# Causal mask of the last twelve head pairs through masked copies of the gate sums, and a new planned order

## The chip, the cores and the metric

The kernel runs on one core of one Trainium2 chip. The metric is the device time of one execution in microseconds (us); the time before is the median of three runs.

## The reference

Two parts follow one another. The first is attention with a forget gate (batch 8, 8 heads, 576 positions, head size 64), the second a gated feed-forward block (4608 tokens, model width 512, inner width 1536):

```python
scores = scale * np.matmul(q, k.transpose(0, 1, 3, 2))
cum = np.cumsum(np.log(np.clip(f, 0.0001, 1.0)), axis=-1)
decay = cum[:, :, :, None] - cum[:, :, None, :]
scores = np.where(causal, -1000000000.0, scores + decay)
scores = scores - np.max(scores, axis=-1, keepdims=True)
attn = np.exp(scores)
attn = attn / (np.sum(attn, axis=-1, keepdims=True) + 1e-09)
attn_out = np.matmul(attn, v)
x = attn_out, heads joined, 4608 x 512
out = (silu(x @ w_gate) * (x @ w_val)) @ w_out
```

`causal` is true above the diagonal: a query sees no later key.

## The kernel before

**The tiles of the work.** Two heads of one batch form a pair; pairs 0 to 31 go through attention one after another, four pairs to a batch of 576 tokens. A pair's 576 queries are nine blocks of 64 rows; the two heads of a pair lie one above the other in the 128 partitions. Block i needs keys 0 to 64(i+1). The nine blocks form two groups: g=0 is blocks 0 to 3, g=1 is blocks 4 to 8.

**Attention of a pair, step by step.** K and Q are loaded (`kf`, `qf`, two buffers each), cast to bf16 with Q scaled by -1/8 (`kb`, `qb`, lines 451, 453; 530 to 534 for the first four pairs), transposed by TensorE (lines 467, 546) and copied out of PSUM to `kt` and `qz` (lines 479, 481; 559, 561). Then line 594 multiplies queries and keys into `sp` (PSUM, two banks), one matmul for each block, or two where a block needs more than 512 columns. **The causal mask** is a second matmul behind it, line 598: the identity as weights times a 128x64 `mask` that holds 1e9 above the diagonal, added to the last 64 columns of the block. VectorE then adds the gate sums `cb` to the scores and keeps the row minimum in one instruction (line 622, `tensor_tensor_reduce` with add and min, into `t` and `tm`; with the signs turned, the minimum stands for the maximum). A reading of its accumulator follows each. ScalarE takes the exponent and the row sum (line 642), VectorE the reciprocal of the sum (lines 656 to 660), GpSimd scales the rows to bf16 `pk` (line 678). `pk` is transposed by TensorE for pairs 0 to 7 (line 708, out of PSUM at 713) and by a DMA for the rest, and line 734 multiplies by V; line 758 writes the result into the ring `xT`.

**The feed-forward block.** Twelve tiles of 256, 256, seven times 512, 256, 128 and 128 tokens. For each tile line 816 makes 96 gate and value matmuls, lines 822 to 827 the activation (one ScalarE and two VectorE instructions of 512 columns per step), line 844 the output matmuls, 851 or 853 the copy to `ot` and 856 the store. A tile can start when all four pairs of its batch have written its tokens to `xT`. `xT` is a ring of `NRING` tokens, and a pair's result waits until the tile whose tokens it overwrites has been through line 816.

**What sets the order.** No engine's order is written out by hand. `Plan.order` takes every operation with its engines, costs, readers and writers, plays the kernel through on a model of engines, buffers and transfers, always starts next what can start first (ties by `prio`), and the instructions are issued on each engine in the order that comes out. Costs in the plan so change no instruction, only its place and sometimes its engine. Transfers are modelled on two wires, one for loads issued by SP and ACT, one for loads issued by GpSimd (POOL). `STARTUP` lists the first loads in order: `pN` the first 256 positions of K and Q (part A) for pairs N and N+1, or the whole K and Q of pair N from 4 on; `kN` and `qN` the other 320 positions (part B); `cN` gate sums; `vBC` chunk C of V of batch B; `wg`, `wv`, `wo` weights. `AHEAD` and `BEHIND` chain a load to one some places in front of it. `HEAD` gives the order of the first eight score groups (pair, group): 00 10 20 30 11 01 31 21. `NUDGE` shifts the priority of single units: aP.G attention of pair P group G, fT and oT the gate and output parts of tile T, qP the preparation of pair P, vB the V of a batch.

**What lies ready in the code.** From pair `MFROM` on, line 598 is left out; `copies` makes `cm`, the sum of `cb` and the mask for all nine diagonal blocks in one 128x576 add on GpSimd or VectorE, and `scores` adds `cb` to the columns left of the diagonal block and `cm` to the diagonal block, two instructions for a block where line 622 made one. `MFROM` is 32 here, so no pair does so. `TWO` sets how the two minima would join: apart with a small GpSimd instruction behind, or chained, the second addition starting from the first one's minimum. Block 8 is over 512 columns wide and so is cut in front of its diagonal block already: its second line-622 instruction is chained, for every pair.

Of the kernel before, what the change touches and what calls it, by code (L numbers as in the profile page):

```python
# [8 lines left out]
F32 = mybir.dt.float32  # L9
# [11 lines left out]
class Op:  # L21
    __slots__ = ("n", "engs", "fn", "reads", "writes", "prio", "lat", "dma", "deps", "start", "end", "eng", "after", "holds", "bias", "ring")

    def __init__(self, n, engs, fn, reads, writes, prio, lat, dma, after, holds):
        self.holds = list(holds)
# [7 lines left out]
class Plan:  # L33
# [24 lines left out]
    def op(self, engs, fn, reads=(), writes=(), prio=0.0, lat=80, dma=0, after=(), holds=()):  # L58
        o = Op(len(self.ops), engs, fn, list(reads), list(writes), prio, lat, dma, list(after), holds)
        self.ops.append(o)  # L60
        return o

    def order(self):
# [7 lines left out]
        for o in self.ops:  # L71
            deps = {d.n: d for k in o.reads for d in writers[k] if d is not o}
# [21 lines left out]
        wire = {True: 0, False: 0}  # L94
# [41 lines left out]
        while ready:  # L136
# [63 lines left out]
def kernel(  # L200
# [11 lines left out]
    nc = tc.nc  # L212
# [16 lines left out]
    NRING = 2560  # L229
# [10 lines left out]
    MFROM = 32  # L240
# [5 lines left out]
    TWO = True  # L246
# [9 lines left out]
    BEHIND = 6  # L256
# [4 lines left out]
    SLACK = 400  # L261
# [3 lines left out]
    STARTUP = "p0 f9 k0 p2 wv0 wg0 c0 v01 q1 q0 wv2 wg2 c1 v02 v00 k2 v04 c3 q2 wv4 v03 wg4 q3 c2 p4 v11 c4 wg8 wv8 c5 v14 p5 v13 v12 p6 c7 v10 c6 wo0 wo4 wo8 p7"  # L265
# [3 lines left out]
    NUDGE = "a5.0:-2 a8.0:1 a13.0:-1 a15.0:-2 a17.0:-2 a18.0:1.5 a22.0:2.5 a23.0:-1 a25.1:-1 a26.1:-1.5 f1:-2 f5:9 f7:0.5 o3:-4.5 o4:-0.5 o6:-8 o7:-3 q8:-2 q13:-3.5 q20:-2 q23:2 q25:4 q26:3.5 q30:-2"  # L269
# [33 lines left out]
    bufs("t", [P, S], F32, 4)  # L303
    for i in range(0, NB, 2):
        bufs(f"e{i}", [P, QB * (i + 2)], F32, 2)
# [59 lines left out]
    def gates(key, parts, np_, prio):  # L365
        x = lambda: pl.buf(key)[0:np_, :]
        for n, (a, z, src) in enumerate(parts):
            loads["f", key, n] = pl.op({"SP": 600}, lambda e, a=a, z=z, src=src: nc.sync.dma_start(out=pl.buf(key)[a:z, :], in_=src),
                                       (), [(key, 0)] + [key] * (n == 0), prio + n * .01, dma=570)
# [8 lines left out]
    for p in range(NDIRECT):  # L378
# [4 lines left out]
          [("fa", 3)], ["cum_dram"], -120, dma=570, lat=0, holds=["fa"])  # L383
# [31 lines left out]
    def load_pair(p):  # L415
# [5 lines left out]
        for name, src, pr in (("k", k, 0), ("q", q, .1)):  # L421
# [4 lines left out]
                (), [(name + "f", p)], (-99 + 3 * p if p < NPB else s - SOON) + pr, dma=1060, after=[sums[p - BACK, 0 if p - BACK >= NPB else 1]] if p >= NPB else [])  # L426
# [545 lines left out]
```

## Time and profile before

| | |
|---|---|
| median of three runs | 418.94 us |
| lowest and highest | 418.35 and 420.63 us |
| span of the profiled execution, first to last instruction | 417.2 us |
| TensorE matmul busy | 398.3 us, 95% of the span |
| VectorE, ScalarE, GpSimd busy | 79%, 74%, 60% |
| mean granted TensorE clock | 0.996 |

The profiled execution has no other time on its page than its span; the median of the runs is 1.7 us above it, and that is taken for what lies around the span. PE is TensorE's matmul row, PEld its weight loads, DVE VectorE, ACT ScalarE, POOL GpSimd, SP the engine that issues most transfers. A PE row's duration runs from issue to the end of the pipeline, so rows overlap; what a matmul takes of the stream is the distance from its start to the next start. The same holds of DVE rows, less strongly.

### The profile page before, as it was taken

Reading aid. Unit: us, or ns where it says so; the run is one execution under the profiler, and the core shown is the slowest. Engines: PE = TensorE matmul, PEld = TensorE weight load, DVE = VectorE, ACT = ScalarE, POOL = GpSimd, SP = SyncE. Lnnn points to the kernel's source line nnn. Section 1 sums busy time; section 2 is a strip of 40 time slices with the busy share of each in tenths; the row PEclk is TensorE's granted clock in tenths of the full one; section 3 lists DMA queues with packets and bytes.
Section 4 is the critical chain, followed back from the end, with each engine's and each line's share of the span. In section 5 each row is a group of like instructions: output and inputs, shape, how many; then the busy total and the mean of one; then the engine's idle time right before and its main releaser. Section 6 shows DMA issues by size and latency. Waiting matters only on the chain.

```text
span 417.2 us, 9955 instructions
## 1 busy us (share of the span) xinstructions
PE 398.3 (95%) x3250; PEld 232.3 (56%) x3296; DVE 328.9 (79%) x1065; ACT 310.3 (74%) x872; POOL 251.7 (60%) x459
## 2 busy tenths in 40 slices
PE   1979999999999999999999999999999999999996
PEld 0636878665555555555555554555555444457675
DVE  5688999999998899989897797798967764565232
ACT  4798999989995999899999984798996533232221
POOL 7589698987887897976968678267773400000000
PEclk9998999999999999999999999999999999999999
DMA  9999979695999999899999999848999211000211
GB/s 183 253 210 225 190 135 252 159 234 141 200 229 215 264 218 236 203 232 222 228 234 218 240 221 223 194 116 190 221 217 186 55 37 50 25 27 25 77 52 52
DMA packets 144004, 71.83 MB, mean 172 GB/s; under 512 B 117904, under 2 KB 131728, under 8 KB 143952
## 3 DMA queue, kind: packets, MB, share of 16 engines
q1 hardware_dynamic: 137568, 65.95, 71.1%
q0 software_dynamic: 5808, 4.72, 7.6%
q10 hardware_dynamic: 576, 0.52, 0.5%
q8 instruction: 26, 0.43, 0.4%
q14 instruction: 26, 0.21, 0.3%
HBM read 46.65 MB, written 9.58 MB: 135 GB/s over the span
## 4 chain that ended last, share of the span: by engine, by line
PE 86%; DVE 4%; issue 1%; ACT 0%
PE gv L816 43%; PE gv L844 22%; PE sp L594 9%; PE tx L734 6%; PE tx L467 3%; PE sp L598 2%; PE gv L708 2%; DVE t L622 1%; DVE pT L713 1%; DVE hh L827 1%; DVE th L824 1%; DVE qz L481 1%; DVE kt L481 0%; ACT ot L851 0%; DVE tm L622 0%
## 5 line engine op out<-in xcount | busy, mean ns | idle before, releaser
L622 DVE CUSTOM_DVE_ANT_0 t<-sp,cb 128x320 f32<-128x320 f32 (+7 forms) x288 | 130.4, 475 | 12.1 <-PE sp L598 8.6
L678 POOL TENSOR_SCALAR pk<-e,lr 128x128 bf16<-128x128 f32 (+3 forms) x190 | 100.5, 533 | 61.8 <-DVE lr L660 16.5
L816 PE MATMUL gv<-xT,wg 128*128 128x512 bf16 (+2 forms) x563 | 110.6, 327 | 0.8
L816 PE MATMUL gv<-xT,wv 128*128 128x512 bf16 (+2 forms) x562 | 109.3, 324 | 0.9
L844 PE MATMUL gv<-wo,hh 128*128 128x512 bf16 (+1 forms) x425 | 104.2, 373 | 0.8
L824 DVE SCALAR_TENSOR_TENSOR th<-th,gv 128x512 f32<-128x512 f32 x108 | 73.9, 684 | 39.3 <-ACT th L822 38.3
L822 ACT ACTIVATE th<-gv 128x512 f32<-128x512 f32 x108 | 64.1, 594 | 44.0 <-PE gv L816 43.1
L642 ACT ACTIVATE e<-t,tm 128x576 f32<-128x576 f32 (+4 forms) x160 | 88.7, 556 | 8.9 <-DVE tm L622 8.3
L827 DVE TENSOR_TENSOR hh<-th,gv 128x512 bf16<-128x512 f32 x108 | 73.7, 685 | 8.7 <-PE gv L816 4.9
L642 ACT ACTIVATE eo<-t,tm 128x128 f32<-128x128 f32 (+3 forms) x128 | 71.1, 556 | 4.7 <-DVE tm L622 2.9
L594 PE MATMUL sp<-kt,qz 128*128 128x448 bf16 (+6 forms) x320 | 71.9, 293 | 1.5 <-DVE tm L622 1.4
L678 POOL TENSOR_SCALAR pk<-eo,lr 128x128 bf16<-128x128 f32 (+3 forms) x127 | 67.6, 532 | 5.4 <-DVE lr L660 3.1
L816 PEld LDWEIGHTS <-wg 128*128 128x128 bf16 x576 | 49.8, 98 | 35.7
L816 PEld LDWEIGHTS <-wv 128*128 128x128 bf16 x576 | 48.9, 98 | 33.7 <-issue 0.3
L844 PEld LDWEIGHTS <-hh 128*128 128x128 bf16 x444 | 39.9, 98 | 39.0
L598 PE MATMUL sp<-mask,ident 128*128 128x64 bf16 x288 | 48.0, 197 | 0.0
L594 PEld LDWEIGHTS <-qz 128*128 128x128 bf16 x320 | 30.9, 100 | 20.9 <-DVE tm L622 0.9
L851 ACT ACTIVATE ot<-gv 128x512 f32<-128x512 f32 (+1 forms) x31 | 17.9, 580 | 27.1 <-PE gv L844 26.2
L598 PEld LDWEIGHTS <-ident 128*128 128x128 bf16 x288 | 27.2, 100 | 12.6 <-issue 1.9
L734 PE MATMUL tx<-pT,vt 128*64 128x320 bf16 (+4 forms) x448 | 29.6, 266 | 1.9 <-DVE pT L713 1.3
L451 POOL TENSOR_SCALAR qb<-qf 72x1024 bf16<-72x1024 f32 x28 | 29.1, 1041 | 3.1 <-DMA qf<-in_q_dram 2.0
L642 ACT ACTIVATION_READ_ACCUMULATOR e<-t,tm 128x1 f32 x160 | 30.6, 192 | 0.0
(69 smaller groups left out, 389.0 us busy)
## 6 DMA issues: line engine op xcount, KB each, us to landing
out_dram<-ot SPq DMA_DIRECT2D x35, 256.0 KB
vf<-in_v_dram SPq DMA_DIRECT2D x32, 256.0 KB
cb<-cum_f SPq DMA_DIRECT2D x56, 144.0 KB
kf<-in_k_dram SPq DMA_DIRECT2D x28, 288.0 KB
qf<-in_q_dram SPq DMA_DIRECT2D x28, 288.0 KB
wo<-in_moe_w_out_dram POOLq DMA_DIRECT2D x3, 512.0 KB, 10.8
vf<-in_v_dram SPq DMA_DIRECT2D x8, 128.0 KB
wv<-in_moe_w_val_dram POOLq DMA_DIRECT2D x2, 512.0 KB, 8.4
```

The lines of the kernel that those rows point to most:

```text
L451: eng[e].tensor_scalar(dst, src, -scale, 1.0, op0=ALU.mult, op1=ALU.mult)
L594: nc.tensor.matmul(sp[:, o:o + z - a], qz[:, i, :, :].rearrange("p h r -> p (h r)"), kt[:, a:z], start=True, stop=not last or p >= MFROM)
L598: nc.tensor.matmul(sp[:, o - QB:o], ident, mask, start=False, stop=True)
L622: nc.vector.tensor_tensor_reduce(out=pl.buf(tk)[:, a:z], in0=pl.buf(sk)[:, o:o + z - a], in1=pl.buf(("cm", p))[:, i, :] if own else pl.buf ...
L642: nc.scalar.activation(pl.buf(ek)[:, :L], pl.buf(tk)[:, :L], AF.Exp, bias=pl.buf(("tm", p, g))[:, 0, i:i + 1], scale=-1.0, accum_out=pl.bu ...
L678: eng[e].tensor_scalar(dst, src, r, 1.0, op0=ALU.mult, op1=ALU.mult)
L734: nc.tensor.matmul(xo[r, 0:QB * n], vt[:, c, 2 * hp + h, :], pT[:, a:a + n, 64 * h:64 * h + 64], start=(c == 0), stop=(c == nch - 1))
L816: nc.tensor.matmul(pl.buf(bk)[:, j * n:j * n + n], wt[:, ko, fc * P:fc * P + P], xT[:, ko, x0:x0 + n], start=ko == 0, stop=ko == KD - 1)
L822: pl.op({"ACT": 487}, lambda e, u=u: nc.scalar.activation(pl.buf(("th", t, u)), pl.buf(("wg", t, u)), AF.Tanh, scale=0.5), [("wg", t, u)], ...
L824: pl.op({"DVE": 605}, lambda e, u=u: nc.vector.scalar_tensor_tensor(pl.buf(("th", t, u)), pl.buf(("th", t, u)), 1.0, pl.buf(("wg", t, u)), ...
L827: pl.op({"DVE": 605}, lambda e, u=u: nc.vector.tensor_mul(pl.buf(("hh", t, u)), pl.buf(("th", t, u)), pl.buf(("wv", t, u))), [("u", t, u), ...
L844: nc.tensor.matmul(pl.buf(bk)[:, 0:z - a], hh[:, (fc % nf) * n + ms * P:(fc % nf) * n + ms * P + P], wo[:, fc, a:z], start=fc == 0, stop=f ...
```

## The change

Pairs 20 to 31 leave out the mask matmuls and use `cm`; the minima are chained. `xT` gets shorter, by 512 tokens, and `cm` gets two buffers. The plan's transfer model is another one, and a number of its settings, the order of the first loads and the priorities differ. The loads of the first four pairs, two transfers each, were one operation of the plan and are now two.

```diff
-    NRING = 2560
+    NRING = 2048
-    MFROM = 32
+    MFROM = 20
-    TWO = True
+    TWO = False
-    BEHIND = 6
+    BEHIND = 4
-    SLACK = 400
+    SLACK = 800
-    STARTUP = "p0 f9 k0 p2 wv0 wg0 c0 v01 q1 q0 wv2 wg2 c1 v02 v00 k2 v04 c3 q2 wv4 v03 wg4 q3 c2 p4 v11 c4 wg8 wv8 c5 v14 p5 v13 v12 p6 c7 v10 c6 wo0 wo4 wo8 p7"
+    STARTUP = "p0 f9 wg2 wv0 p2 v00 k2 q1 wg0 v02 q0 k0 c1 q3 wv2 v01 c2 wg4 q2 v03 wv4 wg8 c3 c0 c6 c4 p4 v04 wv8 p5 p6 v10 c7 c5 v12 wo0 v14 wo4 v11 p7 wo8 v13"
-    NUDGE = "a5.0:-2 a8.0:1 ... q26:3.5 q30:-2"          (28 units)
+    NUDGE = "a0.0:-64.5 a0.1:-2 a1.0:-5 ... a3.0:-7 ... v0:-55.5 v1:10.5 ... v6:1.5"   (85 units)
+    bufs("cm", [P, NB, QB], F32, 2)
```

The plan's transfers; `pk` is a size of the operation's packets, 84 where none is given:

```diff
-                at = max(wire[q], s + (2550 if q else 2000))
-                both = max(0, min(2 * o.dma, wire[not q] - at))
-                wire[q] = at + o.dma + both / 2
-                wire[not q] += both / 2
+                head, tail = (2850, 500) if q else (1500, 1000) if s < 12000 else (2000, 1100)
+                at = max(wire[q], s + head)
+                left_ = max(0, wire[not q] - at)
+                part = o.pk / (o.pk + last[not q])
+                wire[q] = at + min(o.dma / part, o.dma + left_)
+                wire[not q] += min(o.dma, left_ * part / (1 - part))
+                last[q] = o.pk
...
-                o.end = wire[q] + 1100
+                o.end = wire[q] + tail
```

The planned durations of the single transfers are changed with it (K 1060 to 950, Q 1060 to 1240, gate sums 570 to 670, weights and V about a tenth less, and so on).

More of the change, by code (lines that the diff above doesn't have):

```diff
@@ L21, with __init__ @@
 class Op:
-    __slots__ = ("n", "engs", "fn", "reads", "writes", "prio", "lat", "dma", "deps", "start", "end", "eng", "after", "holds", "bias", "ring")
-    def __init__(self, n, engs, fn, reads, writes, prio, lat, dma, after, holds):
-        self.holds = list(holds)
+    __slots__ = ("n", "engs", "fn", "reads", "writes", "prio", "lat", "dma", "deps", "start", "end", "eng", "after", "holds", "bias", "ring", "pk")
+    def __init__(self, n, engs, fn, reads, writes, prio, lat, dma, after, holds, pk):
+        self.holds, self.pk = list(holds), pk
         self.n, self.engs, self.fn, self.reads, self.writes = n, engs, fn, reads, writes
@@ L499, in load_parts, with load @@
             m = (z - a) // r
[L501 to L507 removed]
+            def load(e, u, fk=fk, src=(k if name == "k" else q), a=a, z=z, r=r, m=m):
+                h0 = 2 * (hp + u)
+                (nc.scalar if e == "ACT" else nc.sync).dma_start(
+                    out=pl.buf(fk)[m * u:m * u + m, :, 0:r * D],
+                    in_=src[b, h0:h0 + 2, a:z].rearrange("h (p r) d -> p h (r d)", r=r))
+            loads[name, p, x] = [pl.op({"ACT": 720} if p == 0 and x == "A" else {"SP": 620}, lambda e, u=u, load=load: load(e, u),
+                                       (), [fk], -99 + 3 * p, dma=(z - a) * 2.1, pk=50) for u in range(n)]
         for x, a, z, sel in (("A", 0, CUT, NSELA), ("B", CUT, S, NSEL)):
```

41 lines of the change are left out of this document (17 added, 24 removed).

## The prediction

> **What bounds the kernel now.** I read the page first: busy time by engine, the slices, the chain that ended last.
>
> ```profile
> PE 398.3 (95%) x3250; PEld 232.3 (56%) x3296; DVE 328.9 (79%) x1065; ACT 310.3 (74%) x872; POOL 251.7 (60%) x459
> PE   1979999999999999999999999999999999999996
> DVE  5688999999998899989897797798967764565232
> PE 86%; DVE 4%; issue 1%; ACT 0%
> ```
>
> TensorE is busy in every slice but the first, the third and the last, and 86% of the chain lies on it. VectorE is close behind until slice 30 and half idle afterwards. A busy PE row says little by itself, since rows overlap, so I take the busy time by stretches and look where matmuls wait.
>
> ```profile
> 0.00:10.00 10.00, 0.87 (x5) 0.64 (x6) 5.26 (x13) 4.69 (x7) 7.43 (x33) 1.00 0.90 182
> 10.00:20.00 10.00, 10.00 (x55) 6.25 (x55) 6.06 (x28) 7.25 (x27) 5.88 (x12) 1.00 1.26 251
> 20.00:30.00 10.00, 7.76 (x77) 4.78 (x75) 8.79 (x40) 9.41 (x33) 8.85 (x19) 1.00 0.94 215
> 30.00:40.00 10.00, 8.44 (x72) 6.04 (x71) 8.74 (x32) 8.40 (x23) 9.02 (x16) 0.83 1.13 223
> 40.00:57.20 17.20, 16.96 (x217) 13.89 (x216) 17.15 (x47) 16.02 (x40) 13.13 (x21) 1.00 0.76 156
> 205.00:340.00 135.00, 133.99 (x994) 69.49 (x1012) 111.21 (x365) 105.94 (x306) 85.24 (x152) 1.00 0.88 187
> 340.00:417.20 77.20, 73.59 (x538) 44.94 (x542) 34.29 (x50) 22.15 (x38) 0.00 (x0) 1.00 0.11 42
> ```
>
> The columns are the stretch, its length, then busy time (and count) of PE, PEld, DVE, ACT and POOL, the granted clock, the transfer engines' share and GB/s. Two regimes show. Up to about 57 us the kernel starts up: TensorE lacks work, VectorE, ScalarE and GpSimd are filled to about nine tenths from 20 us on, and from 40 to 57 VectorE hasn't a gap (17.15 of 17.2). Behind that TensorE is full: 133.99 of 135 us in the stretch that holds the pairs to be changed. So a matmul removed there is worth its place in the stream, work of another engine there is worth nothing while it keeps ahead, and the first 57 us are a matter of order.
>
> **The masks removed.** Line 598 goes for pairs 20 to 31, 9 matmuls a pair.
>
> ```profile
> 197.50:330.00 132.50, 17.34 (x108) 9.91 (x108) 1.00 0.94 198
> 236.50 0.33 PE L594 MATMUL sp<-kt,qz 128*128 128x384 bf16 x1
> 236.66 0.19 PE L598 MATMUL sp<-mask,ident 128*128 128x64 bf16 x1
> 236.69 0.30 PE L594 MATMUL sp<-kt,qz 128*128 128x320 bf16 x1
> 236.82 0.19 PE L598 MATMUL sp<-mask,ident 128*128 128x64 bf16 x1
> 236.85 1.03 PE L844 MATMUL gv<-wo,hh 128*128 128x512 bf16 x4
> ```
>
> The first row, of line 598 alone, counts them: 108, with 17.34 us of busy PE. That sum misleads, being latency. The start distances say what one takes: 236.66 to 236.69 and 236.82 to 236.85, so 0.03 us. 108 x 0.03 = 3.2 us off a full stream: **-3.2 us**. The rounding of starts leaves 0.02 to 0.04 us for one (-2.2 to -4.3). The weight load that each brings (9.91 us over 108) stays hidden beside the matmul in front, or the distances could not be 0.03.
>
> The Trainium skill (TensorE: Matmul & The Clock Gate, section Back-to-back issue gap) gives about 81 ns for each matmul in a stream of weight loads and 128-column matmuls. An estimate by that page is 8.7 us for the 108; the trace, with 0.03 us, doesn't bear it out for 64 columns.
>
> **The additions split.** In a pair, seven blocks (1 to 7) get a second line-622 instruction; block 0 is all diagonal, and block 8 is cut already. So 84 more on VectorE.
>
> ```profile
> 25.78 0.28 DVE L622 CUSTOM_DVE_ANT_0 t<-sp,cb,tm 128x64 f32<-128x64 f32 x1 [0.20 <-PE sp L598]
> 25.99 0.62 DVE L622 CUSTOM_DVE_ANT_0 t<-sp,cb 128x448 f32<-128x448 f32 x1
> 26.53 0.69 DVE L622 CUSTOM_DVE_ANT_0 t<-sp,cb 128x512 f32<-128x512 f32 x1
> 27.14 0.08 DVE L622 DVE_READ_ACCUMULATOR2_ANT tm<- 128x1 f32 x1
> ```
>
> Again by starts, accumulator reading included: chained 64 columns 0.21 us, 448 columns 0.54, 512 columns 0.61. A block of 512 becomes 448 and 64: 0.75 for 0.61, so 0.14 more; 84 x 0.14 = 11.8 us of VectorE. From both sides: the listed durations with their readings would make it 0.29 (24 us), a perfectly overlapped second part 0.07 (64 of 448 columns' pace; 6 us). The wait that comes in is that of the second addition for the first one's minimum, on the same engine; behind it stand the next addition, and behind that the exponent on ScalarE, later by 0.14 a block.
>
> **The copies.** Twelve adds of 576 columns, on GpSimd or VectorE, shown nowhere before. Nearest rows:
>
> ```profile
> L824 DVE SCALAR_TENSOR_TENSOR th<-th,gv 128x512 f32<-128x512 f32 x108 | 73.9, 684 | 39.3 <-ACT th L822 38.3
> L453 POOL CAST kb<-kf 96x768 bf16<-96x768 f32 x28 | 22.9, 820 | 1.5 <-PE gv L816 0.8 <-DMA kf<-in_k_dram 0.7
> ```
>
> On VectorE 512 columns with two inputs take 684 ns, so about 0.77 for 576: 9.2 us at most for all. On GpSimd 768 columns with one input take 820 ns, so 0.6 us for 576, and up to double with two: 7 to 15 us. I take GpSimd for most, since it has 135 - 85 = 50 us idle in the stretch, and no wait on them, as the plan makes `cm` ahead of the pair.
>
> What covers these: VectorE is idle for 135 - 111.2 = 23.8 us there, and 11.8 plus at worst 9.2 makes 21.0. It fits, barely in the worst case. If it didn't, attention would end later, and that has a margin too:
>
> ```profile
> 337.35 0.88 PE L734 MATMUL tx<-pT,vt 128*64 128x320 bf16 x14
> 338.10 0.70 ACT L758 CAST xT<-tx 128x320 bf16<-128x320 f32 x2
> 341.62 1.03 PE L816 MATMUL gv<-xT,wg 128*128 128x512 bf16 x4
> 0.00:341.60 341.60, 71.22 (x278) 25.10 (x292) 1.00 0.95 201
> ```
>
> The last pair's result is in `xT` at 338.8 and tile 8, which needs it, starts at 341.62 (tokens 3584 on). The last row is line 844 up to there: 292 of the 336 weight loads of tiles 0 to 7 are done, so 44 output matmuls at 0.22 us (four to 0.86 us) or 9.5 us could run in front of tile 8. So attention may end 2.8 + 9.5 = 12 us later before TensorE runs dry, 9 with its stream 3.2 shorter. **0 us** for additions and copies.
>
> **The shorter ring.** 0. With 2048 tokens the last batch overwrites tokens 1984 to 2560, whose last tile is tile 5.
>
> ```profile
> 34.20:264.00 229.80, 119.10 (x568) 52.07 (x584) 1.00 1.01 214
> 0.00:313.00 313.00, 26.10 (x392) 17.10 (x392) 0.99 0.99 210
> ```
>
> By 264 line 816 has loaded weights 584 times, over the 6 x 96 of tiles 0 to 5; line 734 of pair 28 comes at 313 (28 x 14 = 392 in front of it). 49 us between, so no wait. The seam now cuts eight results in two, some 0.2 us each of an engine with room.
>
> **The first loads.** The transfers move the same bytes; splitting an operation of the plan in two adds none. What moves is which comes first. Now the keys of pairs 2 and 3, part A, come fourth and need a `kf` buffer, of which there are two.
>
> ```profile
> 6.90 1.26 SPq L504 DMA_DIRECT2D kf<-in_k_dram  x2
> 12.90 0.60 POOL L534 CAST kb<-kf 128x512 bf16<-128x512 f32 x1 [1.57 <-DMA kf<-in_k_dram]
> 10.96 0.42 DVE L400 COPY cb<-gv 128x256 f32<-128x256 f32 x1 [1.37 <-PE gv L395]
> 12.65 0.42 DVE L400 COPY cb<-gv 128x256 f32<-128x256 f32 x1 [1.26 <-PE gv L395]
> 14.20 0.42 DVE L622 CUSTOM_DVE_ANT_0 t<-sp,cb 128x256 f32<-128x256 f32 x1 [1.13 <-PE sp L598]
> 16.06 0.75 DVE L561 COPY kt<-tx 128x256 bf16<-128x256 bf16 x2
> 17.70 0.88 DVE L561 COPY qz<-tx 64x256 bf16<-64x256 bf16 x2
> 18.81 0.43 DVE L561 COPY qz<-tx 64x256 bf16<-64x256 bf16 x1
> 34.30 0.41 PE L816 MATMUL gv<-xT,wg 128*128 128x256 bf16 x1
> ```
>
> They are issued at 6.90, when the first buffer comes free, and are cast at 12.90, after GpSimd has waited 1.57 us for them. VectorE meanwhile is idle for 1.37 + 1.26 + 1.13 = 3.8 us, and then makes their copies (0.75 + 0.88 + 0.43 = 2.06 us) between the scores that lead to the first tile, at 34.30. In the new order `p2` stands in front of `k0` and takes the second buffer at once, and parts B of pairs 0 and 1 wait instead. The copies then fit into the idle 3.8 us: **-2.0 us** for the first tile's start. What is late next is part B: pairs 0 to 3 of g=1 must be through for tile 1, at 57 us, and from 40 to 57 VectorE is full. Its work up to there is shifted ahead by the same 2 us, if part B is there. Ends: -3.8 (the idle filled altogether) and +6 (part B late by the 6.0 us that the keys above took from issue to cast); I take -2.0, the row of the copies themselves.
>
> All other shifts (priorities, planned durations, which load follows which) I put at 0 behind 57 us: TensorE there has no idle left to win. The cover is the work that the feed-forward tiles always have ready; without it each wait would count in full.
>
> The sum: 417.2 - 3.2 - 2.0 = 412.0 us of span, with the 1.7 us around it **413.7 us**. The runs' median stands for the same 418.9, the middle of 418.35 to 420.63.
>
> **The rivals.**
>
> *Masks alone.* The copies of `p2` don't get into the gap, as the transfers are shared with `wg2` and `wv0`, now in front: 415.7. For it: the transfer share is 1.26 from 10 to 20 us.
>
> *A better start.* The idle VectorE time is filled whole and the cold stretch shrinks: between 30 and 40 us the granted clock is 0.83, about 1.7 us lost. 417.2 - 3.2 - 3.8 - 1.7 + 1.7 = 410.2. The Trainium skill (TensorE: Matmul & The Clock Gate, section What's actually happening) says that an idle window of about 3.4 us sends TensorE back to half clock; the trace agrees in so far as the 0.83 follows the stretch with only 7.76 of 10 us busy. I also put here, at 0.02 of the chance, that the masks' weight loads count (108 x 0.10 = 10.8 us instead of 3.2); the distances speak against it.
>
> *Eaten up.* Attention of the changed pairs ends late, or the new order leaves TensorE short holes: from 9 us of lateness on, each microsecond counts. If VectorE could be filled only to 0.90, it would have 121.5 us for 111.2 + 21.0 = 132.2, 10.7 late, 1.7 paid; with the start unchanged 417.4, and up to 420 if the holes are as many again.
>
> *Parts B late (slower).* `k0` now stands behind `wg2`, `wv0`, `p2`, `v00`, `k2`, `q1`, `wg0`. If the scores of g=1 begin later by the 6.0 us that a load took, VectorE, full from 40 to 57, can't make it up: tile 0's gate part is done, tile 1 not ready, TensorE idles for them. 418.9 - 3.2 + 6.0 = 421.7. It decides from 3.2 us of lateness. For it: the chain of waits runs on VectorE just there. Against it: the first four groups, all part A, keep VectorE busy until 24 us.
>
> *The change doesn't do what it says*: that line 598 stays for some pairs is excluded by the code, so it has no chance of its own.
>
> **How the numbers follow.** Forecast (412 to 415.4) 0.40; masks alone (415.4 to 416.8) 0.15; better start (below 412) 0.11; eaten up (416.8 to 421.0) 0.17; parts B late (above 421.0) 0.17. A measurement of this kernel can tell about 0.5%, or 2.1 us, from no change: faster means below 416.8, slower above 421.0. So faster 0.66, same 0.17, slower 0.17. The range of 8 in 10 leaves out the slower case and a little at each end: 409.5 to 420.5. The forecast's own range is 412.0 to 415.4.
>
> **What would show it.** Right: line 598 x180 instead of x288; line 622 with 84 more instructions of 64 columns, and VectorE above 120 of 135 us around 205 to 340 without a new idle group on PE; the first gate matmul of line 816 near 32 us instead of 34.3 and tile 1's as much earlier; tile 8's start still behind a finished last pair. Wrong: PE idle groups behind 57 us released by VectorE `tm` or by `xT` (the split's lateness), PE idle between 40 and 60 us released by `kb` or `pT` (parts B), a granted clock under 0.83 in the first 40 us, or `cm` among the releasers of line 622. The forecast also fails if order effects behind 57 us, which I set to 0, are not small.

## The result and the profile after

The changed kernel takes **424.06 us** (median of 6 runs, 421.82 to 426.54) against 420.06 us for the kernel before, run beside it (6 runs, 418.35 to 421.27): ratio **1.0108**, 95% interval 1.0073 to 1.0144. It is slower, where 413.7 us had been forecast. The profiled execution's span is 422.3 us, 5.1 us over the 417.2 of before.

From the page of after: busy time, and the chain that ended last by engine and by line (line numbers are 4 higher than before).

```profile
PE 399.0 (94%) x3188; PEld 230.0 (54%) x3188; DVE 339.8 (80%) x1228; ACT 315.3 (75%) x892; POOL 263.6 (62%) x464
...
PE 65%; DMA 15%; DVE 3%; POOL 2%; ACT 2%; issue 1%; SPq 1%; POOLq 0%; ACTq 0%; DVEq 0%
PE gv L820 32%; PE gv L848 18%; DMA pT<-pk 8%; PE sp L598 6%; PE tx L738 4%; PE tx L471 3%; DMA wo<-in_moe_w_out_dram 2%; DMA kf<-in_k_dram 2%; PE gv L712 1%; DMA cb<-cum_f 1%; DMA qf<-in_q_dram 1%; DVE t L626 1%; POOL pk L682 1%; ACT e L646 1%; DVE th L828 1%
```

TensorE has 108 weight loads less and still holds less of the chain: 65% instead of 86%. Transfers, which held none, now hold 15%, the DMA transposes of the probabilities (`pT<-pk`) alone 8%. The waits of TensorE between 60 and 345 us say the same (engine, line, what was waited for; us in total, times, longest), first before, then after:

```profile
core 0 of [0], span 417.2 us
engine line waited for: us in total, times, longest us
```
```profile
PE tx L738 <- DMA pT<-pk: 3.3, 4, 1.3
PE tx L471 <- POOL kb L457: 1.2, 2, 1.0
PE gv L848 <- DMA wo<-in_moe_w_out_dram: 1.2, 1, 1.2
```

Before the list is empty. After, TensorE waits for four transposes in front of P.V, for two casts of keys (each behind a key load) and for a load of output weights. From its issue to the end of the wait, each of the four transposes takes longer than its plan has it: 8.6, 9.6, 10.1 and 7.6 us for pairs 17, 19, 22 and 29, planned as 7.8, 8.4, 9.7 and 6.5. The windows (stretch, length, busy PE, PEld, DVE, ACT, POOL with counts, clock, DMA share, GB/s) say when; before, then after:

```profile
40.00:60.00 20.00, 19.71 (x258) 16.26 (x257) 19.95 (x61) 18.58 (x50) 14.96 (x23) 1.00 0.82 163
...
180.00:260.00 80.00, 79.41 (x608) 42.02 (x617) 69.79 (x240) 70.74 (x204) 61.12 (x107) 1.00 1.10 227
```
```profile
40.00:60.00 20.00, 17.95 (x233) 14.37 (x230) 19.39 (x62) 19.39 (x54) 17.99 (x30) 1.00 0.91 185
...
180.00:260.00 80.00, 76.43 (x559) 38.87 (x558) 71.44 (x314) 69.11 (x207) 66.13 (x108) 1.00 1.11 224
```

Two stretches lose, then: 40 to 60 us, where VectorE is full in both kernels, and 180 to 260 us, where none of the other engines is full.

### The profile page after: what moved, and what is told of

Read it like the earlier page. It is cut to its first block, busy times and chain, and to the rows that moved or that the text cites. A ratio compares the mean times of both kernels' runs of the same rounds, so it can differ in the third digit from the quotient of the medians.

```text
span 422.3 us, 9974 instructions
## 1 busy us (share of the span) xinstructions
PE 399.0 (94%) x3188; PEld 230.0 (54%) x3188; DVE 339.8 (80%) x1228; ACT 315.3 (75%) x892; POOL 263.6 (62%) x464
## 4 chain that ended last, share of the span: by engine, by line
PE 65%; DMA 15%; DVE 3%; POOL 2%; ACT 2%; issue 1%; SPq 1%; POOLq 0%; ACTq 0%; DVEq 0%
PE gv L820 32%; PE gv L848 18%; DMA pT<-pk 8%; PE sp L598 6%; PE tx L738 4%; PE tx L471 3%; DMA wo<-in_moe_w_out_dram 2%; DMA kf<-in_k_dram 2%; PE gv L712 1%; DMA cb<-cum_f 1%; DMA qf<-in_q_dram 1%; DVE t L626 1%; POOL pk L682 1%; ACT e L646 1%; DVE th L828 1%
## 5 line engine op out<-in xcount | busy, mean ns | idle before, releaser
L626 DVE CUSTOM_DVE_ANT_0 t<-sp,cb 128x320 f32<-128x320 f32 (+7 forms) x276 | 123.4, 466 | 13.1 <-PE sp L598 4.6
L820 PE MATMUL gv<-xT,wv 128*128 128x512 bf16 (+2 forms) x576 | 111.3, 326 | 0.0
L848 PE MATMUL gv<-wo,hh 128*128 128x512 bf16 (+1 forms) x444 | 107.1, 374 | 1.2 <-DMA wo<-in_moe_w_out_dram 1.2
L646 ACT ACTIVATE e<-t,tm 128x320 f32<-128x320 f32 (+4 forms) x160 | 88.8, 556 | 6.0 <-DVE tm L626 5.3
L646 ACT ACTIVATE eo<-t,tm 128x256 f32<-128x256 f32 (+3 forms) x128 | 71.2, 557 | 7.2 <-DVE tm L626 5.5
L598 PE MATMUL sp<-kt,qz 128*128 128x448 bf16 (+5 forms) x320 | 71.9, 295 | 4.2 <-DVE tm L626 3.0
L682 POOL TENSOR_SCALAR pk<-eo,lr 128x384 bf16<-128x384 f32 (+3 forms) x123 | 66.7, 542 | 14.4 <-DVE tm L626 11.4
L855 ACT ACTIVATE ot<-gv 128x512 f32<-128x512 f32 (+1 forms) x36 | 21.0, 583 | 28.7 <-PE gv L848 28.3
L626 DVE DVE_READ_ACCUMULATOR2_ANT tm<- 128x1 f32 x404 | 33.3, 82 | 0.0
L602 PE MATMUL sp<-mask,ident 128*128 128x64 bf16 x180 | 30.6, 200 | 0.0
```

Source lines behind the costliest of these rows:

```text
L598: nc.tensor.matmul(sp[:, o:o + z - a], qz[:, i, :, :].rearrange("p h r -> p (h r)"), kt[:, a:z], start=True, stop=not last or p >= MFROM)
L602: nc.tensor.matmul(sp[:, o - QB:o], ident, mask, start=False, stop=True)
L626: nc.vector.tensor_tensor_reduce(out=pl.buf(tk)[:, a:z], in0=pl.buf(sk)[:, o:o + z - a], in1=pl.buf(("cm", p))[:, i, :] if own else pl.buf ...
L646: nc.scalar.activation(pl.buf(ek)[:, :L], pl.buf(tk)[:, :L], AF.Exp, bias=pl.buf(("tm", p, g))[:, 0, i:i + 1], scale=-1.0, accum_out=pl.bu ...
L682: eng[e].tensor_scalar(dst, src, r, 1.0, op0=ALU.mult, op1=ALU.mult)
L820: nc.tensor.matmul(pl.buf(bk)[:, j * n:j * n + n], wt[:, ko, fc * P:fc * P + P], xT[:, ko, x0:x0 + n], start=ko == 0, stop=ko == KD - 1)
```

## The experiments

**How they are compared.** Executions of one order differ by up to 3 us in their first 140 us, in part by how long the clock is granted at half speed around 30 us (0.50 from 33.1 to 36.4 us in before, 1.00 there in after). So beside the ratio I use two parts of each profiled span: up to the first gate matmul of tile 3 (the 289th weight load on its line, tiles 0 to 2 having 96 each), which is ahead of the changed pairs, and the rest. "Late" is actual start less the start in the kernel's own plan, along TensorE, at its end; it stands where the order and the work are the plan's, and, marked *, for four runs that hold another kernel's planned order with other work in it. "Old order" is the plan of before with the ring of 2048, "new order" that of after, each kept on every engine while the work in it changes; "planned anew" means that the planner ordered the changed work itself. Each ratio is against the kernel before on the same chip.

| run | span | tile 3 | rest | late | ratio, 95% interval |
|---|---|---|---|---|---|
| before | 417.2 | 140.4 | 276.8 | 5.1 | 1 |
| after | 422.3 | 142.0 | 280.3 | 12.4 | 1.0108 (1.0073 to 1.0144) |
| old order: ring of 2048 alone | 415.5 | 138.8 | 276.7 | 3.5 | 1.0015 (0.9989 to 1.0042) |
| old order: masks out | 413.4 | 138.2 | 275.2 | | 0.9956 (0.9933 to 0.9979) |
| old order: masks out, copies | 415.2 | 139.9 | 275.3 | | 0.9978 (0.9953 to 1.0003) |
| old order: masks out, split additions | 427.0 | 140.5 | 286.5 | | 1.0240 (1.0206 to 1.0274) |
| old order: copies and additions | 428.4 | 141.1 | 287.3 | | 1.0264 (1.0238 to 1.0290) |
| old order: first try of that | 428.7 | 140.5 | 288.2 | | 1.0301 (1.0275 to 1.0328) |
| old order: half transposes | 418.4 | 141.1 | 277.3 | 6.3* | 1.0008 (0.9986 to 1.0030) |
| old order: blocks 0 and 8 only | 418.0 | 141.2 | 276.8 | | 1.0003 (0.9981 to 1.0025) |
| new order: masks by matmul | 423.9 | 143.1 | 280.8 | 13.8* | 1.0170 (1.0136 to 1.0205) |
| new order: masks out | 420.6 | 142.4 | 278.2 | 10.6* | 1.0096 (1.0065 to 1.0128) |
| new order: half transposes | 416.9 | 142.9 | 274.0 | 7.0* | 1.0001 (0.9974 to 1.0028) |
| planned anew: after, later landings | 421.4 | 142.5 | 278.9 | 9.7 | 1.0106 (1.0060 to 1.0152) |
| planned anew: new model alone | 423.6 | 142.8 | 280.8 | 8.6 | 1.0183 (1.0148 to 1.0217) |
| planned anew: that, later landings | 423.6 | 143.4 | 280.2 | 8.3 | 1.0172 (1.0145 to 1.0199) |
| planned anew: masks, old model | 424.4 | 140.6 | 283.8 | 9.5 | 1.0197 (1.0152 to 1.0243) |
| planned anew: 5 pairs, old model | 415.3 | 139.1 | 276.2 | 4.1 | 0.9991 (0.9972 to 1.0010) |

**The theories.** A: the new order loses; TensorE takes its work in a fixed order and waits where a landing comes later than the plan had it. B: the copies and the added additions make operations late. C: the plan is fitted so closely that any lateness costs, whatever its source.

### Masks by matmul in the new order

```diff
-                                     start=True, stop=not last or p >= MFROM)
+                                     start=True, stop=not last)
-                    if last and p < MFROM:
+                    if last:
-                    [the two additions of a block, the copies]
+                    [one addition of the whole block, no copies]
```

> The changed kernel's order on every engine, but pairs 20 to 31 keep the mask matmuls, one addition a block and no copies (the copies and the left additions of the plan issue nothing). Theory A (the new plan takes transfers for shorter than they are, and TensorE, which takes its work in order, stands at each landing): the waits for pT and for the keys' casts stay, and 108 mask matmuls of 0.03 us come back, so 425 to 427.5 us, 1.2 to 1.8% over the kernel before. Theory B (the copies and the 84 added additions fill GpSimd and VectorE, and what feeds the transposes is late through them): the waits of TensorE behind 180 us vanish, 419 to 421.5.

Ratio 1.0170, in A's range: the new order is slow with the old work too, and taking copies and additions out doesn't help. B falls as the main cause.

### The ring alone

```diff
-    NRING = 2560
+    NRING = 2048
```

> The kernel before with a ring of 2048 tokens and nothing else; the plan gets eight more copies to the ring and a somewhat other order, with the same planned end. Both theories: the same time as before within 0.5% (418 to 422). If it is slower by more, the shorter ring or a mere reshuffling of the order costs what theory A puts down to the transfers.

Ratio 1.0015, with 1 inside the interval: nothing to see. The seams shift the plan's order from the 15th pair on, but its planned end stays 413.2, and so does the rest (276.7). The runs "in the old order" stand on this one.

### Copies and additions in the old order, first try

```diff
+                if name == "q" and p >= CMFROM:
+                    nc.gpsimd.tensor_tensor(cms[p % 2], pl.buf(("cb", p)).rearrange("r (i c) -> r i c", c=QB),
+                                            maskf.unsqueeze(1).to_broadcast((P, NB, QB)), op=ALU.add)
```

> The order of the run with only the shorter ring, its plan untouched, but pairs 20 to 31 leave out the mask matmuls, split the additions (chained) and make the masked copy on GpSimd, issued ahead of the pair's transposes. Theory A: the 108 masks come off a full stream, 3 us under the run with only the shorter ring, 416 to 418. Theory B: TensorE waits behind 180 us appear here as in the changed kernel, 422 to 425.

A flawed one: the copy stands so early on GpSimd that it takes the gate sums that lay in the buffer before, and the load of the right ones waits for it. Its 1.0301 says nothing of the question; a later run does it properly.

### The new kernel with later planned landings

```diff
-                head, tail = (2850, 500) if q else (1500, 1000) if s < 12000 else (2000, 1100)
+                head, tail = (2850, 500) if q else (1500, 1000) if s < 12000 else (2000, 1900)
```

> The changed kernel with one number of its plan changed: a transfer of SP or ACT behind 12 us is taken to land 0.8 us later (1.9 instead of 1.1 us behind its last byte). Planned end 412.5 instead of 410.6 us. Theory A: TensorE's waits for pT go, actual less planned time falls from 12 us to 5 to 8, so 418 to 421 us. Theory B: the same copies and additions, 423 to 425.

Ratio 1.0106, as after; A's number is missed. Of the waits of TensorE from 60 to 345 us the transposes are gone, and another cast, that of queries, is there:

```profile
PE tx L471 <- POOL qb L455: 2.8, 3, 1.7
```

So the mechanism shows (what is planned later isn't waited for), but the plan ends 1.9 us later and the next wait in line takes what was won.

### Copies and additions in the old order, put in by hand

```diff
+    COPIED = [20, 21, 22, 24, 26, 27, 28, 29, 30, 31]
-                    if last and p < MFROM:
+                    if last and p not in COPIED:
+                    if copied and a < d:
+                        [the part left of the diagonal block, with cb]
-                        in1=... pl.buf(("cb", p))[:, a:z], scale=1.0,
+                        in1=cms[COPIED.index(p) % 2][:, i, :] if copied else pl.buf(("cb", p))[:, a:z], scale=1.0,
```

> The order of before (ring of 2048, as in the run that changed the ring alone) stays on every engine; only for ten pairs (20, 21, 22, 24, 26 to 31; 90 masks) the mask matmuls go, a copy of the gate sums on GpSimd is put into a gap of GpSimd that the plan has between the landing of the gate sums and the pair's first addition (10 x 1.41 us), and 70 additions are split in two chained ones (10 pairs x 7) inside the same place of VectorE's order. The order's own theory (the masks are worth what the prediction gave them, the loss lies in the new order): 90 x 0.03 = 2.7 us less, the additions and copies hidden, so a ratio of 0.992 to 0.997 against before. The rival (the copies or the added additions make the score banks or the exponentials late): a ratio of 1.000 or more, with waits of TensorE for VectorE or GpSimd between 190 and 330 us.

Ratio 1.0264. A's number is missed by far: with the old order held, the swap costs 10.6 us in the rest (287.3 against 276.7). The next three runs say which part.

### The masks left out, alone

```diff
-                    if last and p < MFROM:
+                    if last and p < 20:
```

> The order of before with the ring of 2048; the 108 mask matmuls of pairs 20 to 31 are left out and nothing replaces them, so these pairs see 63 keys too many in each diagonal block. This is the masks' price alone. By the prediction's term 108 x 0.03 = 3.2 us less (ratio 0.992); if TensorE waits there for something else in this order, less than 1 us (ratio over 0.997).

Ratio 0.9956: 1.5 us less in the rest than the ring alone, 2.1 in the span, 0.59% or 2.5 us by the ratios. The predicted 3.2 was somewhat too much, within its own bound of 2.2 if the ratios are taken.

### Additions alone, copies alone

```diff
-                        in1=cms[COPIED.index(p) % 2][:, i, :] if copied else pl.buf(("cb", p))[:, a:z], scale=1.0,
+                        in1=pl.buf(("cb", p))[:, a:z], scale=1.0,
-                nc.gpsimd.tensor_tensor(cms[COPIED.index(p) % 2], ...)
```

> The order of before (ring of 2048), mask matmuls of ten pairs left out and their 70 long additions split in two chained ones, but no copies: the second part adds the unmasked gate sums, so these pairs see 63 keys too many in each diagonal block. If the added VectorE work (70 x 0.21 us more) is what made the copies placed by hand slow, this run is as slow: span 424 to 428, ratio 1.018 or more. If GpSimd's copies were the cause, the span is 413 to 416, ratio under 1.002.

```diff
-                    copied = last and p in COPIED
+                    copied = False
```

> The same, the other way round: mask matmuls of ten pairs left out, the ten copies on GpSimd made in the same gaps but read by nobody, the additions undivided and of the unmasked gate sums. If the added VectorE work is the cause, the copies cost little: span 413 to 416, ratio under 1.002. If GpSimd's copies are (the pack operations of probabilities behind them come later), the span is 420 or more.

Both runs are of ten pairs, so 18 of the 108 masks are still in. The copies cost nothing in the rest (275.3 against 275.2 without them); the split additions cost 11.3 (286.5), though VectorE has room. The windows of 190 to 345 us, without and with the split, and the first wait of TensorE there with it:

```profile
190.00:345.00 155.00, 153.20 (x1032) 77.28 (x1051) 126.16 (x418) 121.03 (x356) 96.28 (x171) 1.00 0.87 185
```
```profile
190.00:345.00 155.00, 148.75 (x1023) 73.44 (x1023) 134.63 (x553) 121.40 (x354) 97.97 (x174) 1.00 0.84 181
```
```profile
PE sp L595 <- DVE tm L630: 4.2, 11, 0.8
```

The list has 4.2 of the 11.3 us; the rest is in delays that it doesn't show. VectorE is idle for 20 us and TensorE waits for it all the same: queries times keys need a bank that an addition has yet to free, and there are two. Where VectorE's idle time lay in the old order shows in its groups of the run with the ring alone, in the same 155 us (idle before, and releaser, in the last column):

```profile
L622 DVE CUSTOM_DVE_ANT_0 t<-sp,cb 128x512 f32<-128x512 f32 (+7 forms) x118 | 52.7, 466 | 3.1 <-PE sp L598 1.6 <-issue 0.5 <-ACT eo L642 0.4
L824 DVE SCALAR_TENSOR_TENSOR th<-th,gv 128x512 f32<-128x512 f32 x46 | 31.5, 685 | 11.8 <-ACT th L822 11.5
```

It idles before the activation (11.8 us) and hardly before the additions (3.1 us). VectorE too takes its work in order: room in front of the activation is none for an addition that stands elsewhere. And split in place, an addition costs more than I had counted. From VectorE's timeline of the run with the additions alone:

```profile
217.76 0.35 DVE L626 CUSTOM_DVE_ANT_0 t<-sp,cb 128x192 f32<-128x192 f32 x1
218.04 0.08 DVE L626 DVE_READ_ACCUMULATOR2_ANT tm<- 128x1 f32 x1
218.16 0.28 DVE L630 CUSTOM_DVE_ANT_0 t<-sp,cb,tm 128x64 f32<-128x64 f32 x1
218.37 0.08 DVE L630 DVE_READ_ACCUMULATOR2_ANT tm<- 128x1 f32 x1
218.37 0.28 DVE L626 CUSTOM_DVE_ANT_0 t<-sp,cb 128x128 f32<-128x128 f32 x1
```

The second part starts 0.12 us behind the reading of the minimum that it is chained to. The two take 218.37 - 217.76 = 0.61 us. Undivided, 256 columns take 0.35 by their starts, here in after:

```profile
206.00 0.42 DVE L626 CUSTOM_DVE_ANT_0 t<-sp,cb 128x256 f32<-128x256 f32 x1
206.35 0.08 DVE L626 DVE_READ_ACCUMULATOR2_ANT tm<- 128x1 f32 x1
```

So 0.26 us more for a block, not 0.14: 70 x 0.26 = 18 us of VectorE. These two runs so price the split in place, not the one of the change, whose plan puts other work between the two parts.

### The new order with nothing in the masks' place

```diff
-                    [the two additions of a block, the copies]
+                    [one addition of the whole block, no copies]
```

> The order of after on every engine, but the mask matmuls of pairs 20 to 31 are left out with nothing in their place: no copies, additions undivided (these pairs see 63 keys too many in each diagonal block). Against after it lacks 96 x 0.14 us of VectorE and 12 copies, and nothing of TensorE. If the order alone is what costs (theory A), the span stays near 422: 419.5 to 422.5. If the added additions and copies still delay the transposes and casts in the new order (theory B), it falls to 414 to 418.

Ratio 1.0096, inside A's range (420.6 us), and only 0.12% under after, where each ratio is known to some 0.3%. In the rests of the profiled executions the two are 2.1 us apart (280.3 and 278.2). So in the order that is planned for them additions and copies cost between nothing and about 2 us. The masks can be priced in this order too, by this run and the one with masks by matmul: 0.74% or 3.1 us by the ratios, 2.6 in the rests (280.8 and 278.2). The order alone, this run against the masks left out in the old order, the same work in both: 1.0096 - 0.9956 = **1.40%, 5.9 us** (7.2 in the spans: 4.2 up to tile 3, of which up to 3 may be chance of the execution, and 3.0 behind). Not all of the first part is chance: tile 3 starts at 138.2 to 141.2 in the eight runs of the old order and at 142.0 to 143.1 in the four of the new one, 2.4 us later on average.

### Half transposes, new order and old

```diff
-                    out=both["pT"][pl.where[tk]], in_=both["pk"][pl.where[kk]].rearrange("p s k -> p (s k)")),
+                    out=both["pT"][pl.where[tk]][:, 0:sum(NSL) if p < 14 else 12, :],
+                    in_=both["pk"][pl.where[kk]][:, 0:sum(NSL) if p < 14 else 12, :].rearrange("p s k -> p (s k)")),
```

> The kernel after, but from pair 14 on each joint transpose of probabilities moves 12 of its 25 blocks only, so that half of the weights that P.V reads are those of an earlier pair: every transpose lands some 3 us earlier than in after and holds the queue of SyncE for less, while every engine has the same order and the same work. Theory A (what TensorE loses in the new order are landings that come later than the plan has them, of the transposes and of the loads queued behind them): the waits for the transposes and for GpSimd's casts go, actual less planned stays under 7 us, span 415.5 to 418.5. Theory C (the order is fitted so closely that any operation that is late by a little costs, whichever it is): other waits come in their place, span 420 or more.

> The control of the half transposes: the same cut (12 of 25 blocks from pair 14 on; half of the weights that P.V reads are those of an earlier pair) in the order of before with the ring of 2048. Theory A: nobody waits for a transpose in that order, so the gain is 0 to 1 us (span 414.5 to 415.5 against 415.5 of the ring alone, ratio 0.998 to 1.002). If shorter transposes help every order by lightening the memory traffic, it gains as in after, 4 to 5 us (span 410 to 411.5).

The profile has the landing of two of the 24 transposes alone, of pairs 9 and 29, and pair 9's is whole in both runs. That of pair 29 in the list of transfers (issue to landing, last number), in after and with the halves; then the waits of TensorE from 60 to 345 us with the halves:

```profile
pT<-pk SPq DMA_TRANSPOSE x1, 7.6
```
```profile
pT<-pk SPq DMA_TRANSPOSE x1, 3.7
```
```profile
PE gv L849 <- DMA wo<-in_moe_w_out_dram: 0.8, 1, 0.8
PE tx L739 <- DMA pT<-pk: 0.3, 1, 0.3
```

The longest of the waits, at pair 22, in after and with the halves:

```profile
248.73 1.03 PE L848 MATMUL gv<-wo,hh 128*128 128x512 bf16 x4
251.09 0.88 PE L738 MATMUL tx<-pT,vt 128*64 128x320 bf16 x14 [1.34 <-DMA pT<-pk]
```
```profile
246.03 1.03 PE L849 MATMUL gv<-wo,hh 128*128 128x512 bf16 x4
246.99 0.88 PE L739 MATMUL tx<-pT,vt 128*64 128x320 bf16 x14
```

P.V follows the four output matmuls by 2.36 us in after and by 0.96 with the halves; in after TensorE stands still for the difference, although output matmuls of tile 4, whose inputs VectorE had finished before, stand only two places behind in its order (they come at 252.19). With the transposes shorter and the same order and work on every engine, the new order gains 6.3 us in the rest (274.0 against 280.3) and stays 7.0 behind its plan instead of 12.4. The old order gains nothing from the same cut (277.3 against 276.7, ratio 1.0008). So lighter traffic is not what helps: the new order waits for landings, the old one doesn't. C falls here, since no other wait of their size came in their place.

### The new model of transfers alone, and with later landings

```diff
+                head, tail = (2850, 500) if q else (1500, 1000) if s < 12000 else (2000, 1100)
+                [and the rest of the new model and durations; nothing else of the change]
```

> The kernel before, with the planner's new model of transfers (two queues in turns, the new lengths) and nothing else of the change: masks by matmuls, the old settings and start, ring of 2560; the plan ends at 416.1 instead of 413.2. If the new model by itself lets transfers be planned too early (theory A in its narrow form), the time that actual falls behind the plan grows along the kernel as in after, by 5 us or more, and the span is 423 or more. If the model is harmless and the fitted settings are what makes it fragile (theory C), it stays at about 4 us as in before: span 419 to 421, ratio 1.004 to 1.010.

```diff
-                head, tail = (2850, 500) if q else (1500, 1000) if s < 12000 else (2000, 1100)
+                head, tail = (2850, 500) if q else (1500, 1000) if s < 12000 else (2000, 1800)
```

> The kernel before with the new model of transfers alone, but each transfer of SyncE and ScalarE behind 12 us planned to land 0.7 us later than that model has it; the plan ends at 417.0 instead of 416.1. If the model's early landings are what its plan loses, actual less planned falls from 7.5 to 4 us and the span is 420.5 to 421.5, less than the 423.6 of the model alone. If the loss comes from the order as such, it stays at 7 us: span 423.5 to 425.

The model alone, with the old work, start and settings, makes the kernel 1.8% slower, though its plan ends 2.9 us later only; by itself this is what A in its narrow form expected. Waits of TensorE from 60 to 345 us, the model alone and with the later landings:

```profile
PE tx L737 <- DMA pT<-pk: 2.3, 2, 1.4
PE tx L470 <- POOL kb L456: 1.3, 2, 1.0
```
```profile
PE tx L470 <- POOL kb L456: 1.8, 3, 0.7
PE tx L737 <- DMA pT<-pk: 0.8, 1, 0.8
```

Landings planned later lessen the waits for the transposes, as in the other such run, and those for the casts grow; the span stays 423.6. So A in its narrow form, that one constant of the model is planned too short, falls twice when that constant is changed.

### The masks planned anew under the old model, twelve pairs and five

```diff
-    MFROM = 32
+    MFROM = 20
-    TWO = True
+    TWO = False
-        if n in ("kb", "qb", "kt", "qz", "cm", "kf", "qf", "cb") or ...
+        if n in ("kb", "qb", "kt", "qz", "kf", "qf", "cb") or ...
+    bufs("cm", [P, NB, QB], F32, 2)
```

> The mask part of the change alone, complete: masked copies and split additions for pairs 20 to 31, planned anew with the planner's model, settings and start of before (ring of 2048; the copies take no shift of their pair's loads). The plan ends at 415.8, 2.6 us later than that of before. Theory A (the plan of the old model keeps its landings, the one of the new model doesn't): TensorE waits for no transposes, actual less planned stays at 3 to 5 us, span 418.5 to 421, ratio 1.003 to 1.010. Theory C (a new order with the added work falls behind its plan whichever model made it): 8 us or more behind, span 424 or more.

> As the run with the masks planned anew under the old model, but for pairs 27 to 31 only (45 masks out, five copies); the plan ends at 412.3, 0.9 us before that of before. Theory A: actual less planned stays at 3 to 5 us, span 415 to 417, ratio 0.996 to 1.002, the candidate for the fastest. Theory C: 420 or more.

Five pairs go as A had it: 4.1 behind plan, ratio 0.9991. Twelve don't: 9.5 behind, 1.0197, and no transpose is waited for. There the lateness is VectorE's. From 60 to 345 us, and one place of it on VectorE, GpSimd and TensorE:

```profile
PE sp L595 <- DVE tm L623: 2.9, 5, 1.0
PE tx L468 <- POOL kb L454: 1.8, 2, 1.0
```
```profile
310.70 1.86 DVE L578 TENSOR_TENSOR cm<-cb,maskf 128x576 f32<-128x576 f32 x1
...
311.09 1.63 POOL L679 TENSOR_SCALAR pk<-e,lr 128x512 bf16<-128x512 f32 x2
...
313.22 0.38 PE L595 MATMUL sp<-kt,qz 128*128 128x512 bf16 x1 [0.78 <-DVE tm L623]
```

A copy on VectorE, 0.71 us in the plan, takes 1.86 just in front of a pair's additions, and TensorE waits behind it. So A holds for the new order, but is no law for every plan: here C has its case, with a VectorE operation as the late one.

### Only the masks that need no added addition

```diff
+    FREED = [p for p in range(8, 32) if p not in (19, 23)]
-                    if last and p < MFROM:
+                    if last and not (p in FREED and i in (0, 8)):
```

> The order of before (ring of 2048); masked copies only for the two diagonal blocks whose addition is by itself anyway (blocks 0 and 8), in 22 pairs from 8 on: 44 mask matmuls go, 22 small copies of 128 columns on GpSimd come into its gaps (0.3 to 0.5 us each), and no addition is split or added. By the run with the masks left out (2.1 us for 108) 44 masks are worth 0.9 us: span 414 to 415, ratio 0.995 to 1.000. If even small copies delay the pack operations, span 415.5 or more, ratio over 1.000.

Ratio 1.0003, the rest 276.8: no gain. At 1.5 us for 108 (from the rest of the run with the masks left out), 44 are worth 0.6 us, which this measurement can't tell from none. Together with the five pairs (0.9991, 0.9972 to 1.0010) that leaves no version that beats the kernel before by what can be measured; both beat after.

## Why the prediction was wrong

Ratios along a path on which one thing changes at a time add up to the result: ring +0.15%, masks out -0.59%, the new order +1.40%, copies and additions within it +0.12%: 1.08% together. With the exchange of masks for copies last, the same sum reads: ring +0.15%, the new order with the old work +1.55%, the exchange within it -0.62%, or 2.6 us less (each step to about 0.5%). So the exchange pays in the order planned for it, nearly as forecast, and the order costs more than it brings.

By the profiled spans the sum missed 10.3 us (422.3 for 412.0). Up to tile 3 it had -2.0 and the executions show +1.6 (142.0 against 140.4); behind tile 3 it had -3.2 and they show +3.5 (280.3 against 276.8). Those 6.7 us behind tile 3 are 3.0 for the order, 2.1 for copies and additions and 1.7 that the masks gave less in the old order, with 0.1 off for the ring; each of these figures is from single executions.

- **The failed step** is "All other shifts (priorities, planned durations, which load follows which) I put at 0 behind 57 us: TensorE there has no idle left to win." That TensorE is full says that nothing is to be won, not that nothing is to be lost. "The cover is the work that the feed-forward tiles always have ready" doesn't hold: ready work stands behind the waiting matmul in TensorE's order and doesn't pass it, as at pair 22, where 1.34 us are lost. Behind tile 3 the order lost 3.0 us instead of 0, and the half transposes show landings as the cause: with them out of the way the rest is 274.0, where the sum had 276.8 - 3.2 = 273.6. I had named this as what would fail the forecast, and gave it a part of one rival at 0.17.
- **The first loads**, -2.0, are the second step that failed. The first gate matmul came where predicted, at 32.1 instead of 34.3, and the half-speed stretch of the clock is gone, but tile 1's came later, by the timelines of before and after:

```profile
58.51 0.27 PE L816 MATMUL gv<-xT,wg 128*128 128x256 bf16 x1
```
```profile
60.05 0.38 PE L820 MATMUL gv<-xT,wg 128*128 128x256 bf16 x2
```

  In the waits of TensorE from 37 to 60 us in after (before: 0.3 us in all), it is mostly VectorE that holds it up:

```profile
PE sp L598 <- DVE tm L626: 1.6, 4, 0.6
PE gv L820 <- DMA wg<-in_moe_w_gate_dram: 0.8, 1, 0.8
PE sp L598 <- DVE qz L485: 0.5, 1, 0.5
```

  The windows up to tile 1, before and after (the third busy time is VectorE's):

```profile
0.00:58.50 58.50, 45.28 (x439) 32.69 (x440) 47.30 (x165) 46.84 (x129) 45.54 (x97) 0.97 0.98 201
```
```profile
0.00:60.05 60.05, 45.97 (x455) 33.91 (x456) 51.03 (x176) 48.56 (x139) 45.96 (x99) 1.00 0.96 199
```

  "Its work up to there is shifted ahead by the same 2 us" was wrong: the new order puts 3.7 us more VectorE work ahead of tile 1 (51.03 against 47.30), of which 2.2 us are three casts of K and Q that GpSimd and ScalarE make in before. That this added work is what delays tile 1 fits the waits, but no run changed it alone. The rival "parts B late" had a late tile 1 too, by 6.0 us and with `kb` or `pT` as releaser; it was 1.5 us, with `tm`. Nor is it shown that the new list of first loads makes the early first tile: the run with the new model alone has the old list and starts it at 32.3 as well, and tile 1 at 60.2.
- **The masks**, -3.2, measured 1.5 to 2.5 in the old order and 2.6 to 3.1 in the new one. The mechanism was right, and these runs can't tell the size from 3.2 for sure.
- **The additions and copies**, 0: nearly right in the order planned for them (nothing to about 2 us), wrong in its reason. "VectorE is idle for 135 - 111.2 = 23.8 us there" is no cover as such; held in the old order, split in place, they cost 11.3 us. The cover had to be made by a new order, and that is the order that lost. So the steps weren't independent, which the sum took them to be.
- **The ring**, 0: right (1.0015, interval 0.9989 to 1.0042).
- The profile after showed my signs of failure in part: idle TensorE behind 57 us, though released by transposes and casts and not by `tm` or `xT`. How much earlier than its use each transpose lands I didn't look up in before, where no wait shows.

What stays open: why the new model's orders wait for landings where the old one's don't. It isn't that its plan leaves less room: P.V starts less than 1 us behind the planned landing of its transpose for 14 of 24 pairs in the plan of before and for 12 in that of after. The four awaited transposes took 0.4 to 1.2 us longer than planned, but planning landings 0.7 or 0.8 us later moved the waits and not the end. Whether the new settings and first loads would lose under the old model too was not run.

## What to carry to other kernels

An engine that is 99% busy under a fixed order is a risk, not a cover: a landing a microsecond late stops it, and ready work behind doesn't help. When a change brings a new order, price the order first: list each wait that the old order just avoids (the transfers with the shortest lead over their use), and test the order with the old work in it. Idle time of an engine covers added work only where it lies next to that work in the engine's own sequence.

## What the runs showed of the hardware

**A two-input add on VectorE and GpSimd's work hold each other.** The copies in after (lowest, median and highest ns):

```profile
L581 POOL TENSOR_TENSOR cm<-cb,maskf x8: 1405/1408/1417, 196.9 to 310.0; 128x576 f32<-128x576 f32 x8
L581 DVE TENSOR_TENSOR cm<-cb,maskf x4: 740/1192/1674, 184.0 to 312.7; 128x576 f32<-128x576 f32 x4
```

On GpSimd, always 1.41 us; I had 0.6 to 1.2. On VectorE 0.74, close to the 0.77 of the prediction, up to 1.67. The timeline of after around the last one:

```profile
312.58 0.69 POOL L682 TENSOR_SCALAR pk<-eo,lr 128x512 bf16<-128x512 f32 x1
...
312.65 1.23 DVE L581 TENSOR_TENSOR cm<-cb,maskf 128x576 f32<-128x576 f32 x1
...
313.25 1.19 POOL L682 TENSOR_SCALAR pk<-e,lr 128x512 bf16<-128x512 f32 x1
...
314.42 0.58 POOL L682 TENSOR_SCALAR pk<-eo,lr 128x384 bf16<-128x384 f32 x1
```

The copy meets a GpSimd instruction that ends at 313.25, and ends 0.63 us behind that; the next GpSimd instruction takes 1.19 instead of the 0.69 of its twin, as if it began when the copy was through. The Trainium skill (SBUF — State Buffer, section SBUF: two separate sides) says that a VectorE instruction with two SBUF inputs and a GpSimd instruction that reads SBUF exclude each other for the whole instruction; these rows agree, with 0.5 us on each side. For 128 columns the GpSimd copy took 0.45 us:

```profile
L960 POOL TENSOR_TENSOR cm<-cb,maskf x22: 445/453/461, 86.3 to 316.2; 128x128 f32<-128x128 f32 x22
```

**A chained minimum has a price of its own**: 0.12 us, at the median of some 70 places in the run with the additions alone, between the reading of the accumulator and the start of the instruction that takes it as its scalar, when nothing stands between them.
